# An attention and MLP kernel: a table of starts and engines in place of a priority table and a list scheduler

## The chip, the cores and the metric

The kernel runs on one core of a Trainium2 chip. The metric is the device time of one execution in microseconds, the median of several runs. A core has five engines that work side by side, each through its own queue of instructions in a fixed order: TensorE (PE, matrix products), VectorE (DVE), ScalarE (ACT), GpSimd (POOL) and SyncE (SP, which here only issues DMA transfers). An instruction waits in its queue until everything that it reads is ready, and all that stands behind it on that engine waits too. So the order of each queue matters, beside what the instructions cost.

## The reference

Attention without a softmax over scores, in the cosFormer form, and an MLP with a gate behind it. The inputs are q, k, v (8 batches, 8 heads, 576 tokens, 64 features, float32), w_in (512 x 2048) and w_out (2048 x 512); the output has 4608 rows of 512.

```python
theta = pi / 2 * arange(S) / S
phi(x) = concatenate([relu(x) * cos(theta), relu(x) * sin(theta)])   # 64 -> 128 features
q_p, k_p = phi(q), phi(k)
kv  = einsum('bhsf,bhsd->bhfd', k_p, v)
z   = sum(k_p over the tokens)
num = einsum('bhsf,bhfd->bhsd', q_p, kv)
den = einsum('bhsf,bhf->bhs', q_p, z) + 1e-6
x   = (num / den), heads side by side, as 4608 x 512
h   = x @ w_in
out = (h * cos(h)) @ w_out
```

## The kernel before, in words

The tokens of a batch are 512 + 64. Attention is done batch by batch; the MLP works on nine chunks of 512 tokens: chunk c takes 512 tokens of batch c, and chunk 8 takes the eight rests of 64 tokens. Batches and chunks overlap: while PE does the MLP of one chunk, DVE, ACT, POOL and the DMA engines prepare the attention of the batch after it.

For one batch the steps are these. The loads (L416, L419, on SP) bring k, v, q as float32. `prep` makes the cosine and the sine features in float16: for each of five token blocks of k and of q and for each of the two feature halves one instruction of 128x512, on ACT (L441) or on DVE (L442). `cast_v` turns v into float16: batches 0 and 1 in twenty half-block pieces on ACT (L455) and DVE (L456), the later batches in three pieces on POOL (L457), of two, two and one blocks. `kv` multiplies k' with v and a column of ones (L468), and its copies are on ACT (L480, L485) and DVE (L482). q' is transposed, by PE (L497, with a copy by ACT at L501 or by DVE at L503) for batches 0 and 1, and by a DMA transpose on SP (L507) for the later ones. `num` (L529) multiplies with kv, and DVE normalises (L545 to L549). x is transposed by PE (L569, copy L573) or by DMA (L579).

For one chunk, layer 1 (L626 for chunks 0 and 1, L658, or with seven products for eight at L762 with its sums at L774) makes h in PSUM; `gate` takes the sine of h + pi/2 on ACT (L599) and multiplies it with h on DVE (L601) into gT. Layer 2 is plain for chunk 0 (L864, additions into ost at L872 and L875); for the others it is a scheme with seven products for eight (L929) with sums of gT before it (L909, L956) and sums into the output tile `ost` behind it (L944). `put` (L825) stores a finished tile from POOL's or SP's queue. Sums of the weights are made once (L887 for w_out, L698 for w_in). PE has filler matmuls at the start (L999), which compute nothing that is used.

The weights are loaded from POOL's queue (L1010 for w_in, L1024 for w_out). Small copies on POOL (`hold`, L1004, L1014, L1029, L1036) write one element per part into a tile that a load will overwrite, so that the load can't start before something else has landed.

What sets the order: every piece of work is added to a `Plan` (L116) as a step with an engine, or with a choice of engines (`either`, used by `prep` in the later batches and by `cast_v`), a cost, and the keys that it reads and writes, from which the dependencies follow. `Plan.run` (L160) takes the table `KEYS`, one priority for each of the 1319 steps, and lets `forward` (L173) simulate the five engines: whenever an engine comes free, the ready step with the smallest key is taken, with a short patience for a step that is not yet ready, with a model of the two DMA rings, and with a rule that the DVE and POOL steps marked `port=True` are not planned at the same time. For a step with a choice, the engine on which it would end first takes it. The steps are then emitted in the order of their planned starts:

```python
        return sorted(st, key=lambda s: (s["start"], s["n"]))
```

All of this happens while the kernel is built. On the chip only the order of each engine's queue is left, with the waits that the dependencies make; no planned start is waited for.

Of the kernel before, what the change touches and what calls it, by code (L numbers as in the profile page):

```python
# [16 lines left out]
KEYS = (  # L17
    -203, -73, 57, 447, -197, -132, -67, -2, 63, 128, 193, 258, 1140, 1280, 1552, 1190, 1839, 2130,
    2538, 2160, 743, 685, 1143, 1623, 701, 785, 1097, 1249, 1298, 623, 1358, 1692, 1252, 747, 1312,
    1859, 1428, 1021, 1007, 827, 1106, 869, 953, 1063, 871, 911, 809, 1105, 970, 1130, 933, 995,  # L20
    1181, 1193, 1156, 1069, 1207, 1188, 1250, 1344, 1346, 1786, 1773, 1876, 1798, 1999, 2034, 1404,
    1416, 1761, 1884, 1949, 1984, 2079, 2092, 2140, 2220, 2263, 2303, 1974, 1987, 2025, 2197, 2253,
    2104, 2203, 2290, 2286, 2399, 2469, 2460, 2573, 2643, 2373, 2486, 2556, 2548, 2660, 2730, 2722,
    2835, 2905, 2635, 2747, 2817, 2809, 2922, 2992, 2984, 3096, 3166, 2896, 3009, 3079, 3071, 3244,
    3508, 3245, 3344, 3421, 3158, 3294, 3596, 3587, 3787, 3925, 3500, 3675, 4539, 3675, 3837, 4028,
    2364, 2406, 3399, 3456, 1929, 1969, 2034, 2466, 2506, 2571, 3942, 4170, 3972, 2518, 2726, 2636,
    2701, 2766, 2831, 3715, 3551, 3841, 3725, 3757, 3613, 3799, 3394, 3673, 4123, 3883, 3887, 4107,
    4241, 4093, 3949, 4153, 4457, 3986, 4061, 4371, 4454, 4412, 4395, 4587, 4745, 4174, 4259, 4541,
    4600, 4387, 4358, 4148, 4321, 4216, 4361, 4185, 4336, 4222, 4310, 4478, 4416, 4552, 4662, 4675,
    4784, 4907, 5080, 4645, 4632, 4669, 4884, 5030, 4930, 5115, 5202, 5374, 5455, 4860, 4872, 4973,  # L30
    5127, 5167, 5349, 5325, 5446, 5569, 5629, 3762, 4011, 3934, 4617, 4198, 4872, 4687, 5265, 4942,
    5324, 5397, 5844, 8555, 8645, 5592, 6104, 6114, 6354, 10004, 10374, 5237, 5405, 5573, 5150,
    5315, 5385, 5765, 5877, 5947, 5852, 6048, 6207, 5939, 6098, 6293, 6026, 6345, 6415, 6286, 6462,
    6590, 6373, 6574, 6651, 6585, 6684, 6754, 6688, 6850, 6920, 6800, 7017, 7095, 6975, 7191, 7261,
    7087, 7250, 7322, 7309, 7474, 7544, 7419, 7608, 7752, 7531, 7718, 7813, 5088, 6476, 8546, 9206,
    4407, 4489, 4572, 4655, 4740, 5025, 5718, 5634, 5802, 5676, 5741, 5505, 5679, 5760, 5567, 5803,
    6156, 6266, 6376, 6461, 6523, 6624, 5933, 5905, 6015, 6020, 6062, 6147, 6165, 6210, 6292, 6148,
    6283, 6553, 6512, 6400, 7271, 6775, 6788, 6815, 7174, 7300, 7062, 7074, 7156, 7396, 7548, 7284,
    7296, 7383, 7618, 7658, 7518, 7506, 7605, 7728, 7768, 6981, 7887, 8432, 6887, 7197, 7893, 7641,
    7751, 8001, 8803, 8678, 8918, 9366, 8097, 8270, 9047, 9488, 9600, 10003, 9117, 9995, 10431,  # L40
    11307, 11397, 10082, 10194, 10298, 13101, 13218, 7838, 8005, 8104, 7924, 8240, 8310, 8010, 8179,
    8249, 8184, 8301, 8371, 8444, 8652, 8742, 8357, 8602, 8681, 8530, 8826, 8917, 9030, 9250, 9320,
    8765, 8876, 9020, 9229, 9416, 9486, 9401, 9706, 9776, 9315, 9519, 9589, 9798, 10062, 10138,
    9884, 10422, 10492, 9687, 10007, 10077, 10282, 10473, 10553, 5950, 5885, 6777, 6712, 6842, 6925,
    7129, 7067, 7831, 7943, 6955, 7502, 7710, 6712, 7350, 7412, 8335, 8445, 8275, 8616, 8852, 8926,
    8055, 8117, 8308, 8385, 8165, 8467, 8062, 8207, 8607, 8540, 8478, 8732, 8764, 8702, 9117, 9018,
    9006, 9081, 9481, 9216, 9204, 9381, 9907, 9587, 9575, 9650, 10203, 9785, 9773, 9837, 10032,
    9970, 10170, 10326, 11655, 9942, 10868, 10962, 11194, 10212, 10627, 10754, 10368, 10517, 10833,
    10710, 10797, 11023, 11576, 10928, 11015, 11578, 11102, 11475, 11894, 11673, 11804, 12365,
    12046, 12375, 12777, 14242, 14152, 12506, 12939, 13341, 16279, 16189, 10929, 11316, 11161,  # L50
    11690, 10666, 11007, 10884, 11100, 11185, 11255, 11245, 11342, 11202, 11292, 11431, 11515,
    11388, 11454, 11678, 11784, 11760, 11994, 12086, 11301, 11628, 11723, 11562, 11944, 12025,
    12177, 12508, 12653, 11891, 12342, 12592, 11978, 12168, 12133, 12252, 12693, 13013, 12263,
    12392, 12331, 12458, 12462, 12531, 12593, 12714, 12793, 12899, 12637, 12743, 12838, 12766,
    13126, 13196, 12680, 13065, 13135, 13088, 13229, 13299, 12853, 13004, 13074, 8178, 8243, 8922,
    8987, 8857, 9052, 8978, 9883, 9945, 10112, 9547, 9644, 10174, 9582, 9821, 9759, 10264, 10094,
    10204, 10455, 10604, 11057, 10236, 10353, 10435, 10647, 10523, 10813, 10771, 10585, 11074,
    10883, 10709, 11394, 10945, 11117, 12202, 11289, 11189, 11349, 12327, 11648, 11661, 11898,
    12452, 12021, 12034, 12147, 12827, 12307, 12319, 12426, 12577, 13373, 13500, 13627, 13411,
    13498, 13676, 13237, 13324, 13835, 14657, 13759, 14089, 14262, 13914, 14244, 14701, 14332,  # L60
    14419, 14771, 14791, 14878, 15125, 17316, 17226, 15250, 15474, 16265, 18948, 19038, 13756,
    13994, 13802, 14161, 13585, 13788, 13629, 13923, 14081, 14194, 13858, 13969, 14002, 14131,
    14045, 14255, 14201, 14316, 14429, 14543, 14617, 14885, 14998, 13673, 14379, 14482, 14506,
    14762, 14832, 15077, 15324, 15428, 14704, 15221, 15291, 14661, 14935, 14965, 15064, 15760,
    15830, 15009, 15109, 15163, 15274, 15207, 15352, 15387, 15489, 15610, 15716, 15431, 15560,
    15655, 15796, 16023, 16093, 15562, 15882, 15952, 15882, 16084, 16154, 15648, 15821, 15891,
    10683, 10748, 11264, 11199, 11329, 11590, 12044, 12280, 11392, 11832, 12218, 11516, 12323,
    11454, 12106, 11770, 12831, 12721, 12941, 13175, 13026, 13616, 12620, 12558, 12702, 12880,
    12942, 13085, 13492, 13257, 13729, 13554, 13726, 13994, 13845, 13907, 14314, 13902, 13846,
    14053, 14529, 14188, 14176, 14377, 15222, 14605, 14592, 14893, 15531, 15065, 15052, 15186,  # L70
    15379, 15362, 15338, 15550, 16902, 16228, 16408, 16688, 16335, 16491, 16737, 16031, 16118,
    16830, 17737, 16820, 16907, 17185, 17038, 17193, 17775, 17410, 17498, 18089, 17869, 18044,
    18314, 19801, 19711, 18304, 18732, 19209, 21700, 21610, 16060, 16375, 16342, 16891, 16291,
    16489, 16447, 16627, 16849, 16924, 16578, 16663, 16776, 16899, 16733, 16985, 16994, 17202,
    17285, 17391, 17125, 17235, 17330, 16621, 17135, 17269, 16205, 17545, 17615, 17653, 17958,
    18028, 17281, 17601, 17676, 17367, 17495, 17739, 17862, 18125, 18211, 17585, 17887, 18000,
    18075, 17957, 18150, 18217, 18375, 18461, 18567, 18261, 18411, 18505, 18131, 18361, 18444,
    17783, 18699, 18778, 18584, 18886, 19008, 18454, 18649, 18839, 12952, 13017, 14249, 14184,
    13929, 14119, 15159, 14985, 14639, 14515, 15047, 14317, 14577, 14823, 14200, 14019, 15539,
    15429, 15649, 15969, 15734, 16342, 15374, 15436, 15656, 15498, 15698, 15781, 16152, 15961,  # L80
    16234, 16018, 16601, 16726, 16539, 16787, 17618, 16435, 16422, 16522, 17428, 16720, 16708,
    17046, 17743, 17181, 17169, 17505, 17948, 17641, 17628, 17923, 18073, 19144, 19271, 19398,
    19279, 19366, 19497, 18919, 19192, 19739, 20160, 19583, 19670, 19799, 19956, 20155, 20259,
    19869, 20043, 20667, 20329, 20529, 20750, 22444, 22534, 20746, 21006, 21724, 24275, 24365,
    18699, 18942, 18745, 18975, 18540, 18749, 18863, 19069, 19547, 19617, 18819, 18936, 19148,
    19447, 19006, 19861, 19540, 19678, 19940, 20046, 20242, 20321, 20440, 19453, 19730, 19800,
    19062, 20209, 20379, 20616, 20741, 20811, 19782, 20985, 21055, 20286, 20371, 20485, 20606,
    20691, 20872, 20441, 20641, 20702, 20807, 20833, 20933, 20877, 20994, 21104, 21210, 21118,
# [27 lines left out]
class Plan:  # L116
# [6 lines left out]
    BUSY = 2.2  # L123
# [36 lines left out]
    def run(self):  # L160
# [3 lines left out]
        for s, a, b in zip(st, start, done):  # L164
            s["start"], s["end"] = a, b
# [1012 lines left out]
```

## Time and profile before

| | |
|---|---|
| Runs | 284.87, 284.94, 286.8 us; median 284.94 |
| Span of the profiled execution | 282.7 us, at a mean granted clock of 0.993 |
| Median less span | 2.2 us |
| Busy: PE, DVE, ACT, POOL | 273.2, 249.0, 207.2, 42.7 us |
| Matmuls | 2619 |
| kv's first product, first product of layer 1, end of the last matmul | 15.51, 21.09, 278.64 us |

The span runs from the first instruction to the end of the last one; the time of a run has some 2.2 us more around it. The busy time of an engine counts the time in which it executes an instruction. A wait is an idle time of an engine whose next instruction is held by another engine or by a transfer. A figure like "x8" behind a row means that neighbouring instructions of one kind are put together in it.

### The profile page before, as it was taken

How to read it: one execution, taken by the hardware profiler on the slowest of the kernel's cores; microseconds unless marked ns; L12 is line 12 of the kernel's file. 1: busy time of each engine (PE TensorE's matmuls, PEld its weight loads, DVE VectorE, ACT ScalarE, POOL GpSimd, SP SyncE). 2: the span in 40 equal slices, each digit the busy share in tenths (PEclk: the TensorE clock that was granted, in tenths of full speed). 3: DMA queues.
4: the chain of work that ended last, by engine and by line, in shares of the span. 5: the costliest groups of instructions: out<-in, count | busy, mean ns of one | idle time of the engine just before them, and what ended most of it. 6: DMA issues, size and time to landing. Idle time of an engine off the chain costs nothing.

```text
span 282.7 us, 6583 instructions
## 1 busy us (share of the span) xinstructions
PE 273.2 (97%) x2619; PEld 209.7 (74%) x2619; DVE 249.0 (88%) x452; ACT 207.2 (73%) x356; POOL 42.7 (15%) x71
## 2 busy tenths in 40 slices
PE   7799999989999999999999999999999999999994
PEld 2568957659866679776888678787876876787783
DVE  2877887999999999999999999999999998985952
ACT  2846799696999996899997979996456466564520
POOL 1420020051040060015005100411011001101100
PEclk9799999999999999999999999999999999999999
DMA  6999999769989999999999999639232101201014
GB/s 208 318 203 249 271 295 304 265 195 240 331 195 232 281 186 312 211 326 205 248 276 286 184 242 321 119 114 209 53 111 78 18 0 49 101 2 56 31 66 148
DMA packets 77598, 53.29 MB, mean 188 GB/s; under 512 B 46080, under 2 KB 75264, under 8 KB 77568
## 3 DMA queue, kind: packets, MB, share of 16 engines
q1 hardware_dynamic: 70048, 39.73, 58.4%
q0 software_dynamic: 6784, 12.59, 17.4%
q10 hardware_dynamic: 736, 0.57, 0.6%
q8 instruction: 20, 0.33, 0.5%
q14 instruction: 10, 0.08, 0.1%
HBM read 36.74 MB, written 9.44 MB: 163 GB/s over the span
## 4 chain that ended last, share of the span: by engine, by line
PE 81%; DVE 9%; DMA 7%; ACT 1%; issue 1%; DVEq 0%
PE M L929 33%; PE M L658 15%; PE M L762 9%; DMA qm<-in_q_dram 7%; PE TR L762 4%; PE TR L658 4%; DVE KQ L442 4%; PE M L626 4%; PE ATT L468 3%; PE ATT L529 3%; DVE gT L601 2%; PE M L864 2%; PE M L497 2%; PE ATT L999 1%; DVE x L549 1%
## 5 line engine op out<-in xcount | busy, mean ns | idle before, releaser
L599 ACT ACTIVATE ch<-M 128x512 f32<-128x512 f32 x90 | 52.7, 595 | 22.9 <-PE M L658 8.5
L929 PEld LDWEIGHTS <-gT 128*128 128x128 f16 x560 | 53.9, 98 | 9.0
L601 DVE TENSOR_TENSOR gT<-M,ch 128x512 f16<-128x512 f32 x83 | 55.0, 684 | 4.3 <-ACT ch L599 3.7
L929 PE MATMUL M<-w_out_sb,gT 128*128 128x256 f16 x448 | 55.9, 273 | 0.0
L658 PE MATMUL M<-xT,w_in_sb 128*128 128x512 f16 x184 | 45.4, 379 | 0.1
L441 ACT ACTIVATE KQ<-qm,CS 128x512 f16<-128x512 f32 x58 | 39.3, 717 | 4.1 <-DMA qm<-in_q_dram 4.1
L441 ACT ACTIVATE KQ<-km,CS 128x512 f16<-128x512 f32 x58 | 39.5, 718 | 0.0
L658 PEld LDWEIGHTS <-w_in_sb 128*128 128x128 f16 x256 | 24.2, 98 | 19.8 <-issue 0.2
L825 POOL DMA_DIRECT2D out_dram<-ost x32 | 17.2, 541 | 114.4 <-DVE ost L944 60.1
L929 PE MATMUL M<-T,S 128*128 128x256 f16 x256 | 31.9, 273 | 0.0
L626 PE MATMUL M<-xT,w_in_sb 128*128 128x256 f16 x256 | 30.2, 272 | 1.5 <-DVE gT L601 1.2
L940 ACT ACTIVATE ost<-M 128x512 f32<-128x512 f32 x32 | 19.0, 595 | 16.9 <-PE M L929 14.1
L457 POOL CAST V<-vm 128x1024 f16<-128x1024 f32 (+1 forms) x18 | 17.1, 988 | 81.4 <-DMA vm<-in_v_dram 50.6
L626 PEld LDWEIGHTS <-w_in_sb 128*128 128x128 f16 x256 | 24.7, 98 | 5.4 <-issue 1.9
L929 PEld LDWEIGHTS <-S 128*128 128x128 f16 x256 | 24.8, 98 | 3.9
L549 DVE TENSOR_TENSOR x<-ATT,rec 128x512 f16<-128x512 f32 x32 | 22.1, 691 | 1.1
L944 DVE TENSOR_TENSOR ost<-M,ost 128x512 f32<-128x512 f32 x24 | 16.4, 685 | 6.8 <-PE M L929 6.7
L762 PEld LDWEIGHTS <-w_in_sb 128*128 128x128 f16 x192 | 18.4, 98 | 4.8
L442 DVE TENSOR_SCALAR KQ<-qm,CS 128x512 f16<-128x512 f32 x22 | 13.4, 637 | 4.9 <-DMA qm<-in_q_dram 4.9
L909 DVE TENSOR_TENSOR S<-gT 128x2048 f16<-128x2048 f16 (+1 forms) x16 | 17.4, 1085 | 0.2
L529 PEld LDWEIGHTS <-qT 128*128 128x128 f16 x320 | 15.3, 98 | 2.5 <-issue 0.5
L774 DVE TENSOR_TENSOR Z<-M,Z 128x512 f32<-128x512 f32 x23 | 15.5, 683 | 0.5 <-PE M L762 0.2
(130 smaller groups left out, 426.0 us busy)
## 6 DMA issues: line engine op xcount, KB each, us to landing
out_dram<-ost POOLq DMA_DIRECT2D x32, 256.0 KB, 3.4
qm<-in_q_dram SPq DMA_DIRECT2D x8, 640.0 KB, 7.2
km<-in_k_dram SPq DMA_DIRECT2D x8, 640.0 KB, 7.4
qm<-in_q_dram SPq DMA_DIRECT2D x8, 512.0 KB, 6.6
km<-in_k_dram SPq DMA_DIRECT2D x8, 512.0 KB, 6.8
vm<-in_v_dram SPq DMA_DIRECT2D x6, 640.0 KB, 7.7
vm<-in_v_dram SPq DMA_DIRECT2D x6, 512.0 KB, 6.2
w_in_sb<-in_moe_w_in_dram POOLq DMA_DIRECT2D x4, 512.0 KB, 9.0
```

The costliest lines, as they stand in the source:

```text
L441: fn = {"ACT": lambda: nc.scalar.activation(out=out_, in_=in_, func=AF.Relu, scale=sc), "DVE": lambda: nc.vector.tensor_scalar(out=out_, i ...
L442: "DVE": lambda: nc.vector.tensor_scalar(out=out_, in0=in_, scalar1=0.0, scalar2=sc, op0=ALU.max, op1=ALU.mult)}
L529: nc.tensor.matmul(bank[hb][:, hh * D1:(hh + 1) * D1], lhsT=a[:, h, :], rhs=z[:, h, :], start=(i == 0), stop=(i == len(parts) - 1))
L549: nc.vector.tensor_tensor(out=split(x16[n][:, hs, :], k), in0=A[:, :, :, 0:D], in1=split(rec[n][:, hs], k).unsqueeze(3).broadcast_to((P, k ...
L599: act(0.5, due, lambda: nc.scalar.activation(out=ch[c], in_=bank, func=AF.Sin, bias=math.pi / 2.0, scale=1.0), [key], [("ch", c)])
L601: mul(due, 0.61, lambda q: q.tensor_tensor(out=dst, in0=bank if len(dst.shape) == 2 else bank.rearrange("p (j s) -> p j s", j=dst.shape[1] ...
L626: nc.tensor.matmul(M1[m][:, jj * 2 * P:(jj + 1) * 2 * P], lhsT=w_in_sb[:, cc, j * P:(j + 1) * P], rhs=X[:, cc, ts], start=(cc == 0), stop= ...
L658: nc.tensor.matmul(M, lhsT=w_in_sb[:, cc, j * P:(j + 1) * P], rhs=X[:, cc, :], start=(cc == 0), stop=(cc == NCT - 1))
L762: nc.tensor.matmul(bank[0][:, j * TH:(j + 1) * TH], lhsT=a(cc, j), rhs=b[:, cc, :], start=(first and j == 0 and cc == 0), stop=(last and j ...
L909: dve(0.07 + 1.07 / NG, due, lambda: nc.vector.tensor_tensor(out=out_[:, sl], in0=a[:, sl], in1=b[:, sl], op=op), rd, wr, port=True)
L929: nc.tensor.matmul(bank[0][:, tt * MH:(tt + 1) * MH], lhsT=a[:, j, tt * P:(tt + 1) * P], rhs=b[:, j, :], start=(first and (apart or tt == ...
L940: act(0.5, due, lambda: nc.scalar.activation(out=dst, in_=view(bank), func=AF.Copy), [bank[1]], dk)
```

## The change

The table `KEYS`, the constants of the model (`LINK`, `SHARE`, `WAKE`, `LAND`, `BUSY`, `PATIENCE`) and the functions `link` and `forward` are taken out. Two tables take their place: `STARTS`, one number for each step (a planned start in hundredths of a microsecond, from a search over the order of each engine that was done elsewhere), and `ENGS`, one letter for each step, its engine. `run` sorts the steps by these starts and picks the function for the engine.

```diff
-KEYS = (
-    -203, -73, 57, 447, -197, -132, -67, -2, 63, 128, 193, 258, 1140, 1280, 1552, 1190, 1839, 2130,
...
+STARTS = (
...
+ENGS = (
+    "DDDPSSSSSSSSGGGGGGGGDAPDDDPADAPDDAPAPDADADDDADADADADDDADADPPADPPDPPAPPDPPAPPDPPAPPDPAPADPAD"
...
 class Plan:
-    LINK = {"PE": 0.12, "ACT": 0.05, "DVE": 0.05, "POOL": 0.1, "SP": 0.0}
-    SHARE, WAKE, LAND = {"HW": 0.40, "SW": 0.56}, {"HW": 1.1, "SW": 1.3}, 1.0
-    BUSY = 2.2
-    PATIENCE = {"PE": 0.1, "ACT": 0.25, "DVE": 0.25, "SP": 0.2}
+    LETTER = {"PE": "P", "ACT": "A", "DVE": "D", "POOL": "G", "SP": "S"}
...
     def run(self):
         st = self.steps
-        assert len(KEYS) == len(st)
-        start, done = self.forward([k / 100 for k in KEYS])
-        for s, a, b in zip(st, start, done):
-            s["start"], s["end"] = a, b
-        return sorted(st, key=lambda s: (s["start"], s["n"]))
+        assert len(st) == len(STARTS) == len(ENGS)
+        order = sorted(range(len(st)), key=lambda n: (STARTS[n], n))
+        place = {n: i for i, n in enumerate(order)}
+        for s in st:
+            assert all(place[d] < place[s["n"]] for d in s["deps"])
+            s["fn"] = {self.LETTER[e]: o[3] for e, o in s["opts"].items()}[ENGS[s["n"]]]
+        return [st[n] for n in order]
-    def link(self, n, u):
...
-    def forward(self, key):
...
```

The function that adds the steps is the same in both files (its lines stand 105 lines further up in the new one), and so are the 1319 steps and what depends on what. What differs is the order on each engine, and the engine of 25 `prep` steps: 13 go from ACT to DVE and 12 from DVE to ACT. The places where the orders differ most:

| Place | Order before | Order after |
|---|---|---|
| Head, ACT | two q copies (L501), then four k preps, with V casts | q and k preps, V casts; q copies around the kv copy |
| Head, DVE | q preps, one q copy (L503), six k preps and six V casts | q preps, six k preps and six V casts, q copy, kv copy, normalisation |
| Loads of batch 1 | hold and load of q and of the second half of v between the loads of w_out | both behind the loads of w_out |
| Batch 2, POOL | two stores, three V casts | stores earlier, V casts as the first in the queue when v lands |
| Batch 2, DVE near the casts | a q prep at the casts, then three gate multiplications | five k preps, a q prep, a gate multiplication |
| Batch 3, POOL and DVE | cast, cast, cast; one prep at the first, two at the third | cast, store, cast, cast; three preps between the first and the second cast |
| Batches 4, 5, 7, POOL | casts together, stores around them | stores between the casts |
| Batch 4, DVE | weight sum L698 elsewhere | weight sum L698 between two casts |
| Batch 6, POOL | stores elsewhere | two stores behind the first cast |
| Tail, all engines | | the same |

## The prediction

> **What bounds the kernel now.** I read the busy shares first, then the forty slices, then busy time by stage, then PE's waits, and last the timelines of DVE and POOL at those waits. The page:
>
> ```profile
> span 282.7 us, 6583 instructions
> PE 273.2 (97%) x2619; PEld 209.7 (74%) x2619; DVE 249.0 (88%) x452; ACT 207.2 (73%) x356; POOL 42.7 (15%) x71
> ...
> PE   7799999989999999999999999999999999999994
> ...
> PEclk9799999999999999999999999999999999999999
> ```
>
> PE is busy for 97% of the span at full clock in all slices but the second; DVE, the next, has 12% to spare. Busy time by stage (stretch, its length, then busy time and count of each engine, granted clock, DMA share, GB/s):
>
> ```profile
> core 0: us, PE busy (x) PEld busy (x) DVE busy (x) ACT busy (x) POOL busy (x), PEclk, DMA share, GB/s
> ...
> 8.60:11.60 3.00, 2.99 (x33) 2.99 (x34) 2.22 (x6) 2.24 (x3) 0.79 (x2) 0.58 1.08 359
> ...
> 24.00:50.00 26.00, 25.81 (x274) 19.81 (x272) 21.18 (x49) 21.84 (x39) 1.66 (x3) 1.00 1.14 286
> ...
> 60.00:85.00 25.00, 23.74 (x249) 18.58 (x247) 24.54 (x41) 21.66 (x39) 6.11 (x8) 1.00 1.03 271
> 85.00:278.60 193.60, 193.60 (x1832) 151.65 (x1830) 178.08 (x301) 143.42 (x246) 26.50 (x40) 1.00 0.67 160
> 278.60:282.70 4.10, 0.04 (x1) 0.00 (x0) 0.50 (x2) 0.00 (x0) 0.00 (x0) 0.94 0.40 134
> ```
>
> From 85 us to the last matmul PE is busy in every one of the 193.60 us: no order can gain there, it can only lose. What an order can win back lies in the head (the first layer 1 product starts at 21.09 us, after transposes at half clock and filler matmuls) and in about 3 us of gaps after it. PE's waits name the largest gap after the head:
>
> ```profile
> engine line waited for: us in total, times, longest us
> ...
> PE M L626 <- DVE gT L601: 1.2, 1, 1.2
> ```
>
> It is at 62.4 us. DVE and then POOL there (start, duration, engine, line, operation, output from inputs):
>
> ```profile
> 59.34 3.02 DVE L442 TENSOR_SCALAR KQ<-qm,CS 128x512 f16<-128x512 f32 x1
> 62.28 0.68 DVE L875 TENSOR_TENSOR ost<-M,ost 128x512 f32<-128x512 f32 x1
> 62.88 1.87 DVE L601 TENSOR_TENSOR gT<-M,ch 128x512 f16<-128x512 f32 x3
> ```
>
> ```profile
> 59.48 2.60 POOL L457 CAST V<-vm 128x1024 f16<-128x1024 f32 x3
> ```
>
> One prep of batch 2 took 3.02 us (the median of its kind is 0.48): it ended just after POOL's three V casts. The gate multiplications queued behind it (L601) came late, and with them PE's next product. It happens again at the same place of batch 3, at 81.13 us (1.23 us) and 82.88 us (0.67), for a PE loss of only 0.23, since no gate was due at once. Later POOL can be the one that waits: at 177.92 a cast took 2.01 us beside an L956 sum on DVE, where 1.06 is usual, and PE lost nothing.
>
> **The change, part by part.** The 1319 steps, their dependencies and the instructions are the same, but for 25 preps that swap ACT and DVE (13 one way, 12 the other). The planned starts are not waited for on the chip; what reaches it is each engine's order. So the sum is one of waits, against the profiled 282.7 us of span plus 2.2 us around it, the median of 284.94.
>
> *PE's work:* 2619 matmuls before and after, 273.2 us busy: 0.
>
> *The head.* Before, ACT copies two transposes of q (L501, 1.02 us each) and DVE one (L503, 0.69) ahead of the k preps; after, these copies come behind the k preps and most V casts. k lands at 10.45 us and the two halves of v at 12.1 and 13.7. DVE then has six k preps (0.41 each in a row) and six V casts (0.26), ACT four preps (0.66) and four casts, and DVE's last cast ends near 10.45 + 2.5 + 1.5 = 14.4, and kv could start there instead of at 15.5. But the fillers L999 stand ahead of kv in PE's queue. The first transpose can start at 8.2 instead of 8.61, since the prep order is turned round; two groups at 0.45 and two at 0.85 us (the durations at full and half clock) end at 10.8; four fillers at 0.43 until the half clock ends at 12.5, and twelve at 0.216, end at 15.1. So kv gains 0.4 of the 1.1 us. One late q copy (0.60) now stands on DVE between the kv copy and the first normalisation, which gives back about 0.2 on the way to the first layer 1 product. Bounds: 0 (all given back) and −0.8 (kv at 14.5, less the 0.2). I take **−0.3**, nearer the fillers' row.
>
> In a sentence aside, the Trainium skill ("TensorE: Matmul & The Clock Gate", "What's actually happening") says that an idle window of about 3.4 us halves the clock; the 0.58 of the row from 8.60 agrees, and since PE still waits for q until 8.2, the half clock stays.
>
> *24 to 50 us.* PE loses 0.2 to 0.3 here. The loads of q (and the second half of v) of batch 1 go behind both w_out loads on POOL's and SP's queues, planned 6 us later. Before, q landed at 36.2 and 38.0 behind k at 31.6 with the DMA engines full (share above 1), so their order matters more than their issue. If q came late, its preps, transposes and batch 1's kv would come late, and PE would stand before layer 1 of chunk 1. The bound for that is 1.0 (half of the 1.8 us between q's two landings); on the other side all the 0.3 may be won. I take **−0.2**.
>
> *Batch 2's casts.* Before they cost PE 1.36 + 0.35 = 1.7 us (the second is the run of small gaps in the 12 us after). After, the two stores leave POOL earlier and the casts start on v's landing (56.3 us); DVE does five k preps, then one q prep, then a gate multiplication in that time. A prep thus meets the casts again, though further from the gate that PE needs. If it is held for one cast (1.06 us) less its own 0.48, nothing is late by more than 0.6; if for all three again, by 2.5. Before, a hold of 2.5 cost PE 1.36 beyond the slack, so PE's loss is the hold less about 1.1, plus the small gaps. I take a hold near two casts: a loss of 0.9 in place of 1.7, **−0.8**; bounds −1.7 (none) and +0.3 (2.0 us, all three casts with a nearer gate).
>
> The Trainium skill ("SBUF — State Buffer", "Who interferes with whom") says that whichever of DVE and GpSimd starts first holds their shared pair of ports for its whole instruction; the 3.02 us agree that one is blocked, but not that it is freed after one instruction. With one cast as the hold, the loss would be nothing and the time 283.3.
>
> *Batch 3's casts.* DVE gets three preps between the first and the second cast, where it had one before and one after. PE lost 0.23; after, 0 to 1.0 (three holds of 0.58, a cast less the prep itself, are 1.7; less the 1.1 of slack 0.6; and 0.35 of small gaps as above). I take 0.4, **+0.2**.
>
> *Batches 4 to 7, and the room elsewhere.* PE never waited here. After, POOL's stores stand between casts in batches 4, 5 and 7 and behind a cast in 6, an L698 sum with two SBUF inputs lies between batch 4's casts, and a store that stands behind a cast waits for v's landing (12.71 us of such waiting was seen at 172.72), so an ost buffer may come free late and the sums L944 that write it stall DVE. I cannot show that any of these reaches PE; from below 0, from above one window of batch 2's kind (1.7) and some small gaps like the 0.1 to 0.15 us after 62 us, in all 2.5. Three to four such gaps: **+0.4**.
>
> *The tail.* 4.10 us after the last matmul, same order: 0.
>
> Sum: 284.94 − 0.3 − 0.2 − 0.8 + 0.2 + 0.4 = **284.2**. One per cent, 2.85 us, is about what a measurement of this kernel can tell from no change: below 282.1 is faster, above 287.8 slower. The forecast's own range is 283.0 (batch 2's casts free, 283.3, and 0.3 more of the head) to 286.0 (one more window of 1.7 paid).
>
> **Rivals.** *It all falls out well:* head −0.8, the second stage −0.3 and 0.3 of what is left around it, batch 2 −1.7, batch 3 −0.23: 281.6. For it: each gap has a named cause, and the order moves exactly those steps. Against it: the fillers are still ahead of kv, and preps are still in the cast windows.
>
> *Slower: the cast windows become PE's waits.* Place: the three V casts of batches 2 to 7. Price: 1.7 us each, batch 2's price. Before, only the first was paid in full and the second at 0.23; the others were covered because no prep with a gate close behind stood in them. With n windows paid, the time is 284.94 − 0.5 − 1.9 + 1.7n: 287.6 for three, 289.3 for four, 292.7 for six. It decides from the fourth on. For it: 25 preps changed engines, DVE is busy for 178 of 193.6 us, and PE has no idle time after 85 us that would soak up a shift. Against it: batches 4 to 7 have most preps on ACT in the new table too, and the one collision seen there (177.9) held POOL.
>
> *It does nothing that can be seen:* PE's 273.2 us of work and the head's landings set the time, gains and losses cancel: 284.9.
>
> **How the numbers follow.** Forecast 0.55, nothing seen 0.07, all well 0.12, cast windows 0.26 (of which four or more windows nearly all). Faster 0.12, same 0.55 + 0.07 = 0.62, slower 0.26. The predicted time is the forecast's, 284.2. The range goes from 282.2 (all well but for the last 0.6) to 289.3 (four windows) and leaves out about 0.1 on either side.
>
> **What would show it.** Head: kv's first product at about 15.1 and layer 1's at about 20.8. Batch 2: the prep beside the casts takes 1 to 2.5 us instead of 3.02, and PE's wait for L601 (its line in the new file) there is under 1 us. After 85 us PE's busy time still fills its stretch to within 0.5 us. Wrong would be: several PE waits of over 1 us for gates or casts after 85 us (the slower rival), a q landing of batch 1 that PE waits for, or a first layer 1 product before 20.3.

## The result, and the profile after

The changed kernel is slower: a median of 287.81 us against 285.45, ratio 1.0087 (95% interval 1.0061 to 1.0112). Measured once more beside the experiments it was 289.12 against 285.23, ratio 1.0103 (1.0071 to 1.0134). Ratios leave out the few executions that took over 1.5% longer than the fastest of their kernel. The forecast of 284.2 had the wrong sign; the time lies above the forecast's own range (283.0 to 286.0), inside the whole range (282.2 to 289.3), and at the prediction's edge between "same" and "slower".

The page of the changed kernel; its profiled execution had a span of 287.2 us and a time of 289.0, which is 1.2 above the median:

```profile
span 287.2 us, 6605 instructions
...
PE 273.6 (95%) x2619; PEld 209.5 (73%) x2619; DVE 250.5 (87%) x453; ACT 205.3 (71%) x355; POOL 41.3 (14%) x71
...
PE   7889999979989998999999999999999999999994
```

PE's work is the same (273.6 us, 273.2 before); nearly all of the 4.5 us by which the span is longer are idle time. By stage, with the columns as in the prediction:

```profile
core 0: us, PE busy (x) PEld busy (x) DVE busy (x) ACT busy (x) POOL busy (x), PEclk, DMA share, GB/s
...
24.00:50.00 26.00, 25.95 (x278) 20.00 (x277) 21.51 (x52) 21.27 (x39) 1.66 (x3) 1.00 1.13 284
50.00:60.00 10.00, 9.65 (x87) 6.85 (x86) 9.93 (x15) 8.61 (x17) 3.90 (x5) 1.00 0.77 258
60.00:85.00 25.00, 22.63 (x242) 18.16 (x242) 23.98 (x43) 21.23 (x38) 3.75 (x6) 1.00 1.05 270
85.00:130.00 45.00, 43.77 (x453) 33.36 (x452) 43.52 (x76) 38.59 (x68) 7.31 (x10) 1.00 0.97 234
130.00:180.00 50.00, 48.81 (x491) 37.40 (x489) 47.37 (x83) 42.41 (x74) 5.78 (x9) 1.00 1.06 228
180.00:230.00 50.00, 50.00 (x470) 39.36 (x469) 46.02 (x81) 33.47 (x59) 7.89 (x13) 1.00 0.45 115
```

PE was idle for 1.26 us between 60 and 85 before, 2.37 now; and between 85 and 180, where it never stood, it is idle for 2.4 us. PE's waits:

```profile
engine line waited for: us in total, times, longest us
...
PE M L521 <- DVE gT L496: 1.8, 1, 1.8
...
PE M L657 <- DVE gT L496: 1.2, 1, 1.2
PE M L824 <- DVE ost L839: 0.9, 1, 0.9
PE M L824 <- ACT ost L835: 0.6, 1, 0.6
```

The first three belong to the V casts of batches 2, 4 and 3. Some lines of the timeline around them, in order of time (start, duration, engine, line, operation; lines of the new file are 105 lower):

```profile
56.70 0.80 POOL L720 DMA_DIRECT2D out_dram<-ost  x1
...
56.91 3.47 DVE L337 TENSOR_SCALAR KQ<-km,CS 128x512 f16<-128x512 f32 x2
...
57.50 2.60 POOL L352 CAST V<-vm 128x1024 f16<-128x1024 f32 x3
...
61.42 0.38 PE L521 MATMUL M<-xT,w_in_sb 128*128 128x256 f16 x2 [1.77 <-DVE gT L496]
...
79.19 0.53 POOL L720 DMA_DIRECT2D out_dram<-ost  x1
...
79.47 2.95 DVE L804 TENSOR_TENSOR gT<-gT 128x2048 f16<-128x2048 f16 x1
79.72 1.61 POOL L352 CAST V<-vm 128x512 f16<-128x512 f32 x2
...
83.07 0.38 PE L824 MATMUL M<-w_out_sb,gT 128*128 128x256 f16 x2 [0.95 <-DVE ost L839]
...
104.07 0.52 POOL L720 DMA_DIRECT2D out_dram<-ost  x1 [1.66 <-DVE ost L839]
...
104.28 2.46 DVE L593 TENSOR_TENSOR WS<-w_in_sb 128x1024 f16<-128x1024 f16 x1
104.58 1.61 POOL L352 CAST V<-vm 128x512 f16<-128x512 f32 x2
...
108.43 0.38 PE L657 MATMUL M<-xT,w_in_sb 128*128 128x256 f16 x2 [1.23 <-DVE gT L496]
```

Each time a VectorE step starts 0.2 to 0.3 us ahead of a run of casts, while GpSimd issues the store just before them, and ends after the last cast: the last k prep of batch 2 takes 3.07 us (0.48 is usual; it is the second of the two in the first line), the sum L804 2.95 (1.22), the weight sum L593 2.46 (0.68). A gate multiplication or an addition into `ost` stands behind it on DVE, and PE's next product waits for that. Counted as the time from one PE step to the next above the usual, PE loses 1.94, 1.11 and 1.40 us there, 4.45 in all, where it lost 1.94 before (1.71 in batch 2, 0.23 in batch 3). In this profile 0.9 more go at 136 to 138 us and 1.1 at 156 to 159, where ScalarE stood at preps for a late k and a late q of batch 6 while copies that PE needs were queued behind:

```profile
137.24 0.72 ACT L336 ACTIVATE KQ<-km,CS 128x512 f16<-128x512 f32 x1 [1.00 <-DMA km<-in_k_dram]
...
137.87 0.58 ACT L835 ACTIVATE ost<-M 128x512 f32<-128x512 f32 x1
...
138.50 0.27 PE L824 MATMUL M<-w_out_sb,gT 128*128 128x256 f16 x1 [0.61 <-ACT ost L835]
```

So there were two theories to test: W, that the loss is made in the windows of the V casts; and L, that it is made by loads that land late in front of preps on ScalarE. A third was that PE's own order costs the time.

### The profile page after: what moved, and what is told of

It is laid out like the page before. It is cut to its first block, busy times and chain, and to the rows that moved or that the text cites. A ratio compares the mean times of both kernels' runs of the same rounds, so it can differ in the third digit from the quotient of the medians.

```text
span 287.2 us, 6605 instructions
## 1 busy us (share of the span) xinstructions
PE 273.6 (95%) x2619; PEld 209.5 (73%) x2619; DVE 250.5 (87%) x453; ACT 205.3 (71%) x355; POOL 41.3 (14%) x71
## 4 chain that ended last, share of the span: by engine, by line
PE 68%; DVE 14%; ACT 6%; DMA 6%; issue 3%; SPq 0%; DVEq 0%; ACTq 0%
PE M L824 27%; PE M L553 11%; PE M L657 7%; PE M L521 5%; DMA qm<-in_q_dram 4%; DVE gT L496 4%; ACT KQ L336 3%; PE TR L657 3%; PE M L759 3%; PE TR L553 3%; PE ATT L363 3%; DVE KQ L337 3%; DVE x L444 2%; DMA km<-in_k_dram 2%; PE ATT L424 2%
## 5 line engine op out<-in xcount | busy, mean ns | idle before, releaser
L553 PE MATMUL M<-xT,w_in_sb 128*128 128x512 f16 x184 | 46.2, 379 | 0.0
L336 ACT ACTIVATE KQ<-km,CS 128x512 f16<-128x512 f32 x57 | 38.6, 719 | 2.4 <-DMA km<-in_k_dram 2.4
L553 PEld LDWEIGHTS <-w_in_sb 128*128 128x128 f16 x256 | 23.9, 98 | 18.6
L521 PE MATMUL M<-xT,w_in_sb 128*128 128x256 f16 x256 | 30.9, 272 | 2.1 <-DVE gT L496 1.8
L521 PEld LDWEIGHTS <-w_in_sb 128*128 128x128 f16 x256 | 24.5, 98 | 6.4 <-issue 2.6
L352 POOL CAST V<-vm 128x1024 f16<-128x1024 f32 (+1 forms) x18 | 16.0, 913 | 86.0 <-DMA vm<-in_v_dram 86.0
L657 PEld LDWEIGHTS <-w_in_sb 128*128 128x128 f16 x192 | 18.2, 98 | 6.7 <-issue 1.9
L424 PEld LDWEIGHTS <-qT 128*128 128x128 f16 x320 | 16.1, 98 | 4.3 <-issue 0.6
L804 DVE TENSOR_TENSOR S<-gT 128x2048 f16<-128x2048 f16 (+1 forms) x16 | 17.3, 1085 | 0.1
L494 ACT ACTIVATE ch<-TR 128x512 f32<-128x512 f32 x18 | 10.8, 598 | 8.9 <-DVE gT L496 3.8
```

Source lines behind the costliest of these rows:

```text
L336: fn = {"ACT": lambda: nc.scalar.activation(out=out_, in_=in_, func=AF.Relu, scale=sc), "DVE": lambda: nc.vector.tensor_scalar(out=out_, i ...
L424: nc.tensor.matmul(bank[hb][:, hh * D1:(hh + 1) * D1], lhsT=a[:, h, :], rhs=z[:, h, :], start=(i == 0), stop=(i == len(parts) - 1))
L494: act(0.5, due, lambda: nc.scalar.activation(out=ch[c], in_=bank, func=AF.Sin, bias=math.pi / 2.0, scale=1.0), [key], [("ch", c)])
L521: nc.tensor.matmul(M1[m][:, jj * 2 * P:(jj + 1) * 2 * P], lhsT=w_in_sb[:, cc, j * P:(j + 1) * P], rhs=X[:, cc, ts], start=(cc == 0), stop= ...
L553: nc.tensor.matmul(M, lhsT=w_in_sb[:, cc, j * P:(j + 1) * P], rhs=X[:, cc, :], start=(cc == 0), stop=(cc == NCT - 1))
L657: nc.tensor.matmul(bank[0][:, j * TH:(j + 1) * TH], lhsT=a(cc, j), rhs=b[:, cc, :], start=(first and j == 0 and cc == 0), stop=(last and j ...
```

## The experiments

**The changed kernel once more** (`after_again`, no edit).

> The changed kernel once more, for a second profile and more times. Theory W (cast windows): PE waits again where a VectorE step is held beside the V casts, in batches 2, 3 and 4, for 1.9, 1.1 and 1.4 us, at the same steps. Rival L (late landings): PE waits again at 137 and 156 us, where ScalarE stands at preps for k of batch 6 and q of batch 6. Where a wait is chance, it is missing here. Time 287 to 288.5 by both.

Median 289.12 us, ratio 1.0103 (1.0071 to 1.0134), more than the 287 to 288.5 that both theories gave. The waits of batches 2, 3 and 4 are there at the same casts: 2.09, 1.97 and 1.40 us. In batch 3 v landed later this time, and the casts held a prep (2.17 us) instead of the sum L804. L's waits are gone (0.08 at 138 us), but batch 6 has a fourth window:

```profile
156.77 0.54 POOL L720 DMA_DIRECT2D out_dram<-ost  x1
...
156.91 2.73 DVE L337 TENSOR_SCALAR KQ<-qm,CS 128x512 f16<-128x512 f32 x1
...
157.31 2.04 POOL L352 CAST V<-vm 128x1024 f16<-128x1024 f32 x2
...
160.30 0.27 PE L657 MATMUL TR<-XS,w_in_sb 128*128 128x256 f16 x1 [1.89 <-DVE Z L669]
```

The windows of batches 2, 3 and 4 recur; that of batch 6 and the late landings are in one of the two profiles each.

**Thin casts, in both kernels** (`before_thin`, `after_thin`). One of the 64 features of v is cast, the rest is left out, from batch 2 on. The line of `cast_v` for POOL:

```diff
-              "POOL": lambda: nc.gpsimd.tensor_copy(out=out_, in_=in_)}
+              "POOL": lambda: nc.gpsimd.tensor_copy(out=out_[..., 0:1], in_=in_[..., 0:1])}
```

> The kernel before with every V cast on GpSimd (batches 2 to 7) cut to one of the 64 features, so that POOL's casts take some 0.1 us instead of 0.6 to 1.06; most of v is thus left out from batch 2 on. Theory W: its two windows cost PE 1.7 and 0.2, so it gains up to 1.9 (a time near 283.5). Rival L, and a third one, that the order on PE itself costs the time: no change over 0.5.

> The changed kernel with the same cut of the V casts on GpSimd; most of v is left out from batch 2 on. Theory W: the three windows' 4.4 us of PE's waits go, the late landings' 2.0 stay; the time falls by 3 to 4.4 to 283.5 to 284.8, and the gap to the kernel before with the same cut is under 1.2. Rival L: the gap of 2.4 stays, the time is over 286. Third rival, order on PE: gap stays and no PE wait explains it.

Before with thin casts: 283.85 us, ratio to before 0.994 (0.9914 to 0.9966). After with thin casts: 282.46, ratio 0.9882 (0.9836 to 0.9929). The first falls by 1.4 us, the second by 6.7 from the 289.12 of the same round: below the 283.5 to 284.8 that W had given, and nearer to the losses at the casts in the second profile (2.09, 1.97, 1.40 and 2.05, in all 7.5) than to the 4.4 of the first. In its trace PE has no loss over 0.5 us after the first products of layer 1. Without long casts the new order has the lower median, by 1.4 us, but the two intervals just overlap, and the trace of `before_thin` has losses that no cast makes (0.67 at 49.7 us, 1.11 between 137 and 140). So the slowdown as a whole is made at the casts. The order on PE is out as its cause, and L as more than a part of it.

**Making the casts wait** (`after_holds`, `after_holds4`). The second has the last line of the table too. In batch 2 the copy waits for the q prep right behind the held k prep, in the other batches for the held step itself.

```diff
+        def pool_cast():
+            behind = {(2, 2): lambda: qp[0:1, 2, 0, 1, 0:1],
+                      (3, 4): lambda: G2[1][0:1, 0, 0, TH:TH + 1],
+                      (4, 4): lambda: WSA[2][0:1, 0, 0:1],
+                      (6, 2): lambda: qp[0:1, 4, 0, 0, 0:1]}
+            if (b, t) in behind:
+                nc.gpsimd.tensor_copy(out=V1[0:1, t, 0, 0:1], in_=behind[b, t]())
+            nc.gpsimd.tensor_copy(out=out_, in_=in_)
...
-              "POOL": lambda: nc.gpsimd.tensor_copy(out=out_, in_=in_)}
+              "POOL": pool_cast}
```

> The changed kernel, whole output, with three tiny copies on GpSimd that make a V cast wait for the VectorE step that it would have held: in batch 2 all casts behind the sine prep of q block 2, in batch 3 the second cast behind the sum L804 into gT, in batch 4 the second cast behind the second sum L593 of w_in. The order of every other engine is the same, the casts run up to 1 us later. Theory W: the held steps take 0.5, 1.2 and 0.7 us instead of 3.1, 2.9 and 2.5, PE's three waits shrink from 4.4 to under 1 in all, the time is 284 to 285.3. Rival L: 287 or more. If the casts' lateness itself matters, PE waits before the kv products instead.

Median 284.94, ratio 0.997 (0.9936 to 1.0005). PE's losses in batches 2 and 4 are gone. In batch 3 0.67 us stay, and mostly not by a cast: a prep on DVE waited 1.25 us for a DMA transpose. Batch 6 still cost 2.05.

> The changed kernel, whole output, with the three waits of the run before and a fourth: in batch 6 the second V cast waits for the cosine prep of q block 4, which it held for 2.7 instead of 0.5 us in two profiles, at a PE loss of 2.05. Theory W: that loss goes, the time falls from 284.9 to 283 to 284, below the kernel before by 0.4 to 0.8%. Rival L: PE then waits at the same place for ScalarE, which stands at preps for a late q, and the time stays at 284.9.

Median 284.05, ratio 0.9962 (0.9939 to 0.9985). The wait in batch 6 is gone from the trace; in the ratio the fourth wait is worth only 0.001, and the two intervals overlap, so its gain in time is not shown. In this trace PE lost 1.71 us at 112.6 instead, where a DMA transpose of q came late. The same order, with four tiny copies added, goes from 1% slower to 0.4% faster than before.

**The preps on ScalarE** (`after_best`: the four waits and this).

```diff
+MOVE = {891: 13160, 906: 14820, 910: 14822, 903: 15045}
+STARTS = [MOVE.get(n, t) for n, t in enumerate(STARTS)]
```

> The same four waits, and four preps moved on ScalarE's order: one k prep of batch 6 behind the copies L835 and L665 that PE needs, three q preps of batch 6 behind such copies. Rival L in part: where k or q of batch 6 lands late, PE no longer waits; worth 0 to 1.8 in a run, up to 0.5 in the median. Theory W alone: the same time as the kernel with the four waits, within 0.4.

Median 283.09, ratio 0.994 (0.9912 to 0.9968). 0.96 below the run without the edit, but the two intervals overlap, and the trace of `after_holds4` has no loss at these preps; that late landings cost some tenths of a per cent is possible and not shown.

**The same remedy for the kernel before** (`before_hold`: `pool_cast` with only `(2, 0): lambda: qp[0:1, 1, 0, 1, 0:1]`).

> The kernel before, whole output, its order unchanged, with one tiny copy on GpSimd that makes batch 2's first V cast wait for the sine prep of q block 1 which it held for 3.02 us. Theory W: the prep takes 0.5, PE's waits of 1.36 + 0.35 there go, the time falls by 1.2 to 1.7 to 283.6 to 284.1, as with the thin casts (283.85). If the time of before came from elsewhere: no change.

Median 283.64, ratio 0.9941 (0.9923 to 0.9958). The window of batch 2 now reads:

```profile
60.06 0.47 DVE L442 TENSOR_SCALAR KQ<-qm,CS 128x512 f16<-128x512 f32 x1
...
60.67 0.18 POOL L456 COPY V<-KQ 1x1 f16<-1x1 f16 x1 [0.47 <-DVE KQ L442]
...
61.02 2.04 POOL L457 CAST V<-vm 128x1024 f16<-128x1024 f32 x2 [0.18 <-ACT KQ L441]
61.05 1.27 DVE L606 TENSOR_TENSOR gT<-M,ch 128x512 f16<-128x512 f32 x2
```

The prep takes 0.47 us instead of 3.02, and the gate multiplications, which read one input from PSUM, run beside the casts at their usual pace. PE loses nothing there. With its one window mended, the old order is as fast as the new one with four mended (283.64 against 283.09 and 284.05).

**Shorter casts** (`after_small`, `after_halves`, `before_small`). Four casts of two heads (or two of four) in place of one:

```diff
-              "POOL": lambda: nc.gpsimd.tensor_copy(out=out_, in_=in_)}
+              "POOL": lambda: [nc.gpsimd.tensor_copy(
+                  out=out_[:, i:i + 2], in_=in_[:, i:i + 2]) for i in range(0, H, 2)]}
```

> The changed kernel, whole output, with every V cast on GpSimd cut into four casts of two heads each, of some 0.15 to 0.3 us. Is a VectorE step freed after one GpSimd instruction, or only when GpSimd pauses? By the first the held steps take some 0.3 us more than their own time, PE's waits in batches 2, 3, 4 and 6 shrink from 1.4 to 2 each to under 0.3, the time is near 284. By the second the steps are held for the whole run of casts as before (2.5 to 3 us or more), and the time is 288 to 290.

> The changed kernel, whole output, with every V cast on GpSimd cut into two casts of four heads each (some 0.3 and 0.55 us). Is the hold set by the length of one cast, or does GpSimd go on until a fixed share of its queue is done? By the first the held steps take up to 0.6 us more than their own time, PE's waits are under 0.4 each and the time is 283.5 to 285. By the second the held steps take 2.5 to 3 us again and the time is 287 to 290.

> The kernel before, whole output, its order unchanged, with every V cast on GpSimd cut into four casts of two heads each. Theory W: its hold in batch 2 falls from 3.0 to some 0.7 us, the time by 1.2 to 1.7 to 283.6 to 284.1; the changed kernel with the same cut (283.4) is then as fast or up to 0.7 faster, so that the table by itself is worth that much. Rival: short casts help the new order only (no change here, 285.3), or by something other than the hold.

In quarters the changed kernel takes 283.41 us, ratio 0.9942 (0.9913 to 0.9972), and the steps that were held take 0.5 to 0.7 us. In halves it takes 286.04, ratio 0.999 (0.9951 to 1.0029), between the two answers expected; in batch 2 a prep is held through all six half casts (3.45 us), in batches 4 and 6 only for 0.1 to 0.3. The kernel before gains nothing from quarters: ratio 0.9996 (0.9977 to 1.0015). Its profiled execution took 290.98 us, so only this stretch of it is read:

```profile
60.36 3.24 DVE L442 TENSOR_SCALAR KQ<-qm,CS 128x512 f16<-128x512 f32 x1
...
60.50 3.94 POOL L457 CAST V<-vm 128x256 f16<-128x256 f32 x12
```

Here a prep that starts 0.14 us ahead of the casts is held through eight of the twelve, for as long as by three whole ones. So neither answer that I had put up is right: a hold does not have to end with one instruction, and cutting the casts mends one order and not the other.

**Quarters and the moved preps** (`after_small_act`).

> The changed kernel, whole output, with the cut casts and the four preps of batch 6 that were moved on ScalarE's order behind copies that PE needs. Theory W with the late landings as the rest: 282.4 to 283.4, at or below the best so far (283.09). If the move of the preps did nothing: 283.4, as with the cut casts alone.

Median 283.16, ratio 0.991 (0.9886 to 0.9934), the best ratio of the versions that compute all; against quarters alone (0.9942) the intervals overlap again.

**The head alone** (`head_after`: the table's order for the 92 steps with planned starts before 21.3 us, then the order and engines of the kernel before).

> The order and engines of the table up to the first products of layer 1 (the 92 steps with planned starts before 21.3 us), then the order and engines of the kernel before; whole output. It tells what the head alone is worth. My prediction had -0.3 (0 to -0.8). If the head gives what PE's first product of layer 1 showed with the clock at full speed (20.4 against 21.27): 284.4 to 284.8, with batch 2's window as before. If the gain of the head is given back later: 285.3.

Median 285.71, ratio 0.9998 (0.9976 to 1.0021): it is worth nothing that can be measured. Layer 1 begins at 20.76 us in its profile, and PE loses 0.74 before 49.31 us at a block of layer 2 whose part of w_out lands at 49.18. The old order loses the same 0.75 there in `before_hold` (layer 1 at 20.43) and 0.67 in `before_thin` (21.27), and nothing in the first profile, where this part landed at 48.61. So behind the old order's loads the landing of w_out can take an early start back. In the two profiles of the changed kernel, which loads the rest of batch 1 later, that part landed at 47.40 and 45.88 and PE lost nothing there; what the head is worth ahead of the rest of the table this run doesn't show.

## Why the prediction was wrong

*What bounds the kernel*, that PE has nothing to win after 85 us and can only lose, was right: all the new loss but 0.1 us lies between 58 and 160 us. *PE's work at 0* was right.

The step that failed is the price of the V cast windows. It was wrong in three terms, *batch 2*, *batch 3* and *batches 4 to 7*, which were to bring -0.2 together and brought +4.6 in the first profile and +5.8 in the second.

*The head at -0.3* came out at +0.1 in the first profile. Kv began at 15.31 (15.1 forecast), 0.2 earlier than before, but the way from there to layer 1 was 0.28 longer, and layer 1 began at 21.17 against 21.09. With TensorE at full clock in the head it began at 20.40 in the second profile of the changed kernel. But the old order's full-clock profiles spread from 20.43 (`before_hold`) to 21.27 (`before_thin`), and the new order's to 21.42 (`after_halves`); in the latest of each PE stood for 0.85 and 0.92 us for a part of w_in. So a gain of 0.3 drowns in what differs between executions. What was late next was not asked.

*24 to 50 us at -0.2* held in the first profile (gaps of 0.4 instead of 0.6 us) and not in the second (0.7).

*Batch 2 at -0.8* is a term that failed. I took a hold of two casts and a loss of 0.9; the hold was three casts (3.07 us), the loss 1.94 and 2.09, so the term is +0.2 to +0.4, at or just past the bound that I had given. PE also needed the gate behind the held step sooner: 2.2 us after the step's start instead of 2.9. And the two stores were not gone when the casts came, as the table of the change and the prediction have it: the first waited for an addition into `ost`, they left POOL from 56.10 to 57.50, v landed at 57.00 meanwhile, and the casts followed directly.

*Batch 3 at +0.2* failed: 1.11 and 1.97 instead of 0.23, so +0.9 and +1.7 against a top of +0.8. I had counted three preps and overlooked the sum L804, which reads two inputs from SBUF too, is 1.22 us long, and has an addition behind it that PE needs. In the second profile it was a prep that I had counted, but held for 1.69 us through two casts where I had priced 0.58.

*Batches 4 to 7 at +0.4* is the term that decided. I had named the sum L698 (L593 now) between batch 4's casts, but the 0.4 held only small gaps and no window, because PE had never waited there. The sum cost 1.40 in both profiles; batch 6's prep cost 2.05 in one, and the late landings 2.0 in the other. With a few small gaps that is +3.5 and +3.7 against a top of +2.5.

*The rivals.* The slower one is what happened: V cast windows paid for at 1.1 to 2.1 us each (1.7 forecast), three in one profile and four in the other. Its sums for three and four windows, 287.6 and 289.3, lie near the two medians, in part by luck: the 2.0 us of late landings in the first profile are not in them. I had given it 0.26 and held against it that the later batches have their preps on ScalarE; but sums on VectorE fall into the windows as well. I had also put the free windows of the kernel before down to there being no prep with a gate close behind. That is not the reason: a prep at 125.70 and the sum L956 at 177.80 started 0.23 and 0.12 us ahead of casts there and were not held at all (the last section shows what set these casts apart). The question to ask was how far the order keeps the two apart. The table does: by its planned starts the held steps end 2.1, 2.5, 0.2 and 0.5 us before the casts of batches 2, 3, 4 and 6 that held them. On the chip nothing enforces it. VectorE ran 1.3 us behind its plan in batch 2, 3.2 in batch 3 and 4.4 in batch 4, while the casts that held it were 1.0 and 0.3 ahead in the first two, and only 3.9 behind in batch 4. The planned gaps closed, and the four copies that turn them into waits bring the time back.

The Trainium skill ("SBUF — State Buffer", "Who interferes with whom") says that the one of VectorE and GpSimd that comes first locks the shared ports for its whole instruction. By that rule no hold by a cast is longer than one cast, 1.06 us, and the rule's sum in the prediction was 283.3. The traces agree on who collides (preps, sums with two SBUF inputs; not the gates) and disagree on the length: 3.07 us through three casts. The measurement decides. Who came first is less plain than the start of the casts makes it look, since GpSimd was already issuing a store when each of the steps that were held through a whole run began.

## What to carry to other kernels

An order that keeps two engines apart by planned time alone does not keep them apart: here VectorE drifted by 1.3 to 4.4 us from the plan, and a collision that the plan avoided by 2 us came true in both profiles. Make such a gap a dependency (a copy of one element is enough), or keep the contending steps off one of the engines. Look also at what the other engine does just ahead of the collision, not only at the colliding instruction. And before crediting an order with an earlier start, look for the next landing that it will meet.

## What the runs showed of the hardware that I had not expected

How long a VectorE step is held depends on where it starts. In the twelve traces with V casts on GpSimd of whole size or cut, every held step that started while a cast was running was delayed by 0.05 to 0.79 us, that is by no more than a cast. The ten that started 0.13 to 0.40 us ahead of a run of whole casts and were held were delayed by 1.7 to 2.3 us by two casts and by 2.5 to 2.7 by three: by the whole run.

But not all that start so close ahead are held. The sum L956 of the kernel before kept its 1.22 us, and the cast took 2.01 where 1.06 is usual, so that two casts took 3.01:

```profile
177.80 1.22 DVE L956 TENSOR_TENSOR gT<-gT,S 128x2048 f16<-128x2048 f16 x1
...
177.92 3.01 POOL L457 CAST V<-vm 128x1024 f16<-128x1024 f32 x2 [4.59 <-DMA vm<-in_v_dram]
```

For the hold at 59.34 in the same trace, POOL's row just ahead of the casts is this one:

```profile
58.33 1.15 POOL L825 DMA_DIRECT2D out_dram<-ost  x2 [20.06 <-DVE ost L875]
59.48 2.60 POOL L457 CAST V<-vm 128x1024 f16<-128x1024 f32 x3
```

This separates all cases with whole casts. The ten held steps all started while GpSimd was issuing a store, with the casts directly behind the store. Eleven other preps and steps with two SBUF inputs were running when casts began that GpSimd had waited to start (for v's landing, for PE or for a tiny copy); all eleven kept their usual time, and the first cast took 0.74 to 2.01 us instead of 0.61 or 1.05. With cut casts behind a store, two of nine such steps were held (by 2.76 and 2.97 us), the others delayed by 0.04 to 0.29. If this is what decides, the new order's stores ahead of and between the casts are part of what made its windows dear. It is read off the traces; no run moved a store alone, and the reason was not found.

TensorE's half clock in the head belongs to the execution and not to the kernel: it shows in both first profiles (mean clock 0.993 and 0.991), and not in the second profile of the changed kernel nor in those of the thin casts (0.999 and 1.000). The idle time of PE ahead of its first transpose does not decide it: it was 1.96 us in both first profiles, and 2.23 and 2.35 in `after_thin` and `head_after`, which ran at full clock behind it.
